# Feature sums of the keys on GpSimd instead of VectorE, in a linear-attention and gated-GLU kernel

## The chip, the cores and the metric

The kernel runs on one core of one Trainium2 chip. The metric is device time in microseconds (us) of one execution; lower is better. Engine names are those of the profile: PE (TensorE, matrix products), PEld (its weight loads), DVE (VectorE), ACT (ScalarE), POOL (GpSimd), SP (SyncE, which issues DMAs).

## The reference, cut to what matters

```
x  = A_x                                     # 1 x 2048 x 512, bf16
xn = layernorm(x)
q, k, v = split(xn @ wqkv)                   # 32 heads of 16
pq, pk  = q @ w_phi, k @ w_phi               # per head, 16 features
phi_q = concat(softmax(pq), softmax(-pq))    # 32 features a head
phi_k = concat(softmax(pk), softmax(-pk))
kv, z = phi_k^T @ v, sum over tokens of phi_k
o   = (phi_q @ kv) / (phi_q @ z + 1e-6)
A   = o @ wo
B   = ((xn @ w_gate) * (xn @ w_up)) @ w_down   # 512 -> 1792 -> 512
out = x + A + B
```

The feature sums are the denominators of the softmaxes. For a tile of 128 tokens there are 32 heads x 2 signs = 64 sums of 16 exponentials each.

## The kernel before

Tokens lie in 16 tiles of 128, one token per partition. All SBUF data lie in one big tensor, which the profile calls arena; all PSUM data in ps, eight banks of 128 x 512 float32.

The stages, as the code records them:

- Layer norm of each tile (`emit_ln_stats`, `emit_xn`): DVE makes statistics (L412, L414), GpSimd adds the epsilon and raises to the power -0.5 (L418, L420), DVE normalises (L434). Tiles 0 to 7 are transposed by PE, tiles 8 to 15 by DMAs on SP (L438).
- Keys. `k_pe` makes the values of a tile; `k_pk` multiplies the normalised tile by a weight in which w_phi is already folded, so that a bank of PSUM holds all 512 features. `emit_exp` copies the bank twice, plain and negated, into one of four slots of the staging ring `pst` (two ACT operations, L276), takes the maximum over the 16 features by a tree of four DVE operations (L474: 512, 256, 128, 64 wide), subtracts it (L480, 1024 wide) and takes the exponential on ACT, into `ek`, 1024 bf16 values per token. `k_norm` then adds up the features by `emit_sums`, takes the reciprocal on DVE (L518) and multiplies the exponentials by it (L521, 1024 wide).
- `emit_sums` is a tree of four additions on halves (L494): 1024 values to 512, to 256, to 128, to 64, each group of 16 features by itself. The inputs of the first are bf16; the partial sums are float32 and lie in the same `pst` slot that the tile's features were in, so a slot becomes free for the tile four places later only when its tree is done.
- `emit_kv`, in two halves of eight tiles, multiplies the transposed normalised key features by the values (and a column of ones, for z): 64 products with 65 columns each. The second half needs all 16 tiles of keys.
- Queries (`q_pk`, `q_scale`, `q_T`, `q_num`, `q_oT`): the same exponentials and the same `emit_sums`, then a ratio, a transposition by DMA, and the products with kv.
- GLU: 56 units (4 groups of 512 tokens x 14 blocks of 128 columns). In `glu` PE makes gate and up, four products each, in two of the banks 5, 6 and 7; ACT copies the gate to SBUF, and DVE multiplies the up bank by it (L543).
- `final` adds for every tile the 14 down products and the 4 with wo in one bank, and DVE adds x (L640).

The order on each engine is not the order of the code. Every operation is recorded with its engine, what it reads and writes, and an estimated cost (`dve`: 65 ns plus 1/0.96 ns per element at rate 1; `pool`: 130 + 1.8 ns per element). Dependencies follow from overlapping addresses. `_order` is a list scheduler: it always starts the operation that can start first by these costs, and among several for one engine the one of the smallest priority number. Matrix products of the GLU have late priorities, so they fill PE's gaps; ACT copies and DVE products of the GLU have the most urgent (-1). The result is one fixed list for each engine. Each engine works its list strictly in order; an operation waits on semaphores for its producers, those on the same engine too (except on PE).

Other instructions named later: L394 makes a block-diagonal weight on GpSimd at the start, four products of 128 elements. L596 to L599 scale the queries. L559 to L566 finish kv. The two lines that set a cost for DVE and for GpSimd:

```python
return sc.step(DVE, fn, reads=reads, writes=writes, cost=fixed + rate * n / 0.96, lat=150.0, prio=prio)   # fixed=65
return sc.step(POOL, fn, reads=reads, writes=writes, cost=fixed + rate * n, lat=120.0, prio=prio)          # fixed=130, rate=1.8
```

Of the kernel before, what the change touches and what calls it, by code (L numbers as in the profile page):

```python
# [8 lines left out]
ALU = mybir.AluOpType  # L9
# [187 lines left out]
def _build(nc, es, A_x, A_wqkv, A_w_phi, A_wo, B_w_gate, B_w_up, B_w_down, out):  # L197
# [59 lines left out]
    def sbv(name, lo, n):  # L257
        off = layout[name] + lo
        return arena[:, off:off + n]
# [25 lines left out]
    def dve(fn, reads, writes, n, rate=1.0, fixed=65.0, prio=None):  # L285
        return sc.step(DVE, fn, reads=reads, writes=writes, cost=fixed + rate * n / 0.96, lat=150.0, prio=prio)
# [196 lines left out]
               func=ACTF.Exp)  # L483
        return i % 4

    def emit_sums(e_in, pslot, slot):

        sm = sums_v[:, slot, :]
        part = sbv("pst", pslot * 1024, 1024).bitcast(F32).rearrange("p (g k) -> p g k", g=16)
        src = e_in.rearrange("p (g k) -> p g k", g=16)  # L490
        k = 32
        while k >= 4:
            dst = part[:, :, 0:k] if k > 4 else sm.rearrange("p (g k) -> p g k", g=16)
            dve(lambda e, dst=dst, src=src, k=k: e.tensor_tensor(out=dst, in0=src[:, :, 0:k], in1=src[:, :, k:2 * k],  # L494
                                                                 op=ALU.add), [src[:, :, 0:2 * k]], [dst], 16 * k)
            src = part
            k //= 2
        return sm

    ek_v = sbv("ek", 0, NT * 1024).rearrange("p (t j) -> p t j", t=NT)  # L500

    p_slot = {}
# [10 lines left out]

    def k_norm(t):
        slot = t % 3
        sm = emit_sums(ek_v[:, t, :], p_slot["k", t], slot)
        rs = rs_v[:, slot, :]
        dve(lambda e: e.reciprocal(out=rs, in_=sm), [sm], [rs], 64, rate=6.0)  # L518
        e4 = ek_v[:, t, :].rearrange("p (g f h) -> p g f h", g=16, f=16)
        r4 = rs.rearrange("p (g h) -> p g h", g=16)  # L520
        dve(lambda e: e.tensor_tensor(out=e4, in0=e4, in1=r4[:, :, None, :].to_broadcast([128, 16, 16, 4]),  # L521
                                      op=ALU.mult), [ek_v[:, t, :], rs], [ek_v[:, t, :]], 1024, rate=0.5)
# [67 lines left out]
    def q_scale(t):  # L590

        slot = t % 3
        sm = emit_sums(eq(t), p_slot["q", t], slot).rearrange("p (g w h) -> p g w h", g=8, w=2)
        rf = rsf_v[:, slot, 0:32].rearrange("p (g h) -> p g h", g=8)
        rs = rs_v[:, slot, 0:32].rearrange("p (g h) -> p g h", g=8)
        dve(lambda e: e.reciprocal(out=rf, in_=sm[:, :, 1, :]), [sm], [rf], 32, rate=6.0)  # L596
        dve(lambda e: e.tensor_tensor(out=rs, in0=sm[:, :, 0, :], in1=rf, op=ALU.mult), [sm, rf], [rs], 32)  # L597
        e1 = eq(t).rearrange("p (g w f h) -> p g w f h", g=8, w=2, f=16)[:, :, 1, :, :]
        dve(lambda e: e.tensor_tensor(out=e1, in0=e1, in1=rs[:, :, None, :].to_broadcast([128, 8, 16, 4]),  # L599
                                      op=ALU.mult), [e1, rs], [e1], 512, rate=0.5)  # L600
# [60 lines left out]
    for b0 in range(0, NT, 4):  # L661
        if b0 < 12:
            ln(b0 + 4, 4)
        if b0 == 8:
            load_wT(0, 0.0).deps.append(sc.by_eng[SP][-2])
            emit_kv(0)
            some_glu(99, 2)
        for t in range(b0, b0 + 4):
            k_pk(t)
            k_norm(t)  # L670
            if b0 < 8:
                some_glu(2, 1)
        if b0 < 12:
            for t in range(b0 + 4, b0 + 8):
                k_pe(t)
        if b0 == 8:
            wprime(0)
# [165 lines left out]
```

## Time and profile before

| what | value |
|---|---|
| median of 3 runs | 226.76 us (226.38 to 228.73) |
| the profiled execution | 227.26 us |
| its span, first to last instruction | 225.5 us |
| granted TensorE clock | 0.999 |
| busy PE / DVE / ACT / POOL | 218.9 / 191.7 / 115.5 / 10.2 us |
| all `emit_sums` additions on DVE (L494) | 128 instructions, 49.3 us, mean 397 ns |
| maxima on DVE (L474) | 128 instructions, 31.5 us, mean 272 ns |
| GLU products on DVE (L543) | 56 instructions, 37.9 us, mean 679 ns |
| first sum of the keys, last multiply of the keys starts | 26.34 us, 113.3 us |

How to read it: busy times of different engines overlap. Instructions of one engine overlap a little too (the recorded length of a DVE instruction is longer than its distance to the next), so both the mean length and the distance between starts are used, and it is said which. A row of section 2 has 40 slices of 5.64 us. "Idle before" a group is the time its engine stood still just ahead of it, and the name behind the arrow is what ended the wait.

### The profile page before, as it was taken

What the parts mean: (1) busy time and instruction counts of PE and PEld (TensorE: products, weight loads), DVE (VectorE), ACT (ScalarE), POOL (GpSimd) and SP (SyncE); (2) the same over time, 40 slices, a digit from 0 to 9 for tenths busy, and PEclk for the clock granted to TensorE, in tenths of its full rate; (3) what the DMA queues carried; (4) which work ended last, traced back from release to release, by engine and by line L of the source; (5) the groups of instructions that cost most, each with busy time, mean ns of one, the idle gap of its engine ahead of it and who ended that gap; (6) DMA issues with size and microseconds to landing.
All of it is one profiled execution on the core that took longest, in us unless ns stands there. A gap on an engine that the chain in (4) does not pass through costs nothing.

```text
span 225.5 us, 3619 instructions
## 1 busy us (share of the span) xinstructions
PE 218.9 (97%) x1312; PEld 106.9 (47%) x1312; DVE 191.7 (85%) x548; ACT 115.5 (51%) x193; POOL 10.2 (5%) x29
## 2 busy tenths in 40 slices
PE   8899999999999999998999999989999999999995
PEld 8454444444455454443454444444444444454443
DVE  4758999999993899999989999989999999974121
ACT  2579976674434998654519765536453333100000
POOL 4721000000020000000000000000000000000000
PEclk9999999999999999999999999999999999999999
DMA  6999931300004400000000044434456643663201
GB/s 163 327 269 400 357 119 28 70 0 0 0 3 95 93 3 0 0 0 3 0 1 3 8 89 89 92 67 78 93 57 110 133 115 76 145 140 73 70 23 48
DMA packets 44210, 19.39 MB, mean 86 GB/s; under 512 B 35232, under 2 KB 43168, under 8 KB 44192
## 3 DMA queue, kind: packets, MB, share of 16 engines
q1 hardware_dynamic: 43664, 19.14, 34.5%
q8 instruction: 10, 0.16, 0.3%
q10 hardware_dynamic: 528, 0.02, 0.1%
q14 instruction: 8, 0.07, 0.1%
HBM read 8.67 MB, written 2.10 MB: 48 GB/s over the span
## 4 chain that ended last, share of the span: by engine, by line
PE 66%; DVE 20%; DMA 5%; SPq 5%; issue 2%; ACT 1%; DVEq 0%
PE ps L296 66%; DVE arena L494 4%; DVE arena L543 4%; DVE arena L474 4%; SPq L163 3%; DMA arena<-in_A_x_dram 3%; DVE arena L480 3%; DMA arena<-arena 2%; SPq L164 1%; DVE arena L412 1%; ACT arena L276 1%; DVE arena L613 1%; DVE arena L518 1%; DVE arena L599 0%; DVE arena L521 0%
## 5 line engine op out<-in xcount | busy, mean ns | idle before, releaser
L296 PE MATMUL ps<-arena 128*128 128x512 bf16 (+4 forms) x1312 | 218.9, 330 | 3.9 <-ACT arena L276 1.1
L296 PEld LDWEIGHTS ps<-arena 128*128 128x128 bf16 x1312 | 106.9, 100 | 115.7 <-ACT arena L276 6.0
L276 ACT ACTIVATE arena<-ps 128x512 bf16<-128x512 f32 (+1 forms) x160 | 84.2, 601 | 47.2 <-PE ps L296 42.3
L276 ACT ACTIVATE arena<-arena 128x1024 bf16<-128x1024 bf16 x32 | 34.3, 1074 | 32.0 <-DVE arena L480 31.1
L494 DVE TENSOR_TENSOR arena<-arena 128x512 f32<-128x512 bf16 (+3 forms) x128 | 49.3, 397 | 0.1
L543 DVE TENSOR_TENSOR arena<-ps,arena 128x512 bf16<-128x512 f32 x56 | 37.9, 679 | 3.4 <-PE ps L296 1.8
L474 DVE TENSOR_TENSOR arena<-arena 128x64 bf16<-128x64 bf16 (+3 forms) x128 | 31.5, 272 | 1.7 <-ACT arena L276 1.6
L640 DVE TENSOR_TENSOR arena<-ps,arena 128x512 bf16<-128x512 f32 (+2 forms) x17 | 11.0, 653 | 12.6 <-PE ps L296 12.5
L480 DVE TENSOR_TENSOR arena<-arena 128x1024 bf16<-128x1024 bf16 x32 | 21.7, 677 | 0.0
L412 DVE BATCH_NORM_STATS2 arena<-arena 128x6 f32<-128x512 bf16 x16 | 10.6, 683 | 4.4 <-DMA arena<-in_A_x_dram 4.4
L521 DVE TENSOR_TENSOR arena<-arena 128x1024 bf16<-128x1024 bf16 x16 | 10.9, 681 | 0.0
L613 DVE TENSOR_TENSOR arena<-ps,arena 128x512 bf16<-128x512 f32 x16 | 10.8, 672 | 0.1
L612 DVE RECIPROCAL arena<-ps 128x32 f32<-128x32 f32 x16 | 5.5, 342 | 4.6 <-PE ps L296 4.5
L518 DVE RECIPROCAL arena<-arena 128x64 bf16<-128x64 f32 x16 | 8.7, 546 | 0.1
L434 DVE TENSOR_SCALAR arena<-arena 128x512 bf16<-128x512 bf16 x16 | 6.2, 416 | 1.9 <-issue 1.5
L599 DVE TENSOR_TENSOR arena<-arena 128x512 bf16<-128x512 bf16 x16 | 6.6, 411 | 0.0
L420 POOL TENSOR_TENSOR arena<-arena 128x1 f32<-128x1 f32 (+1 forms) x7 | 5.4, 777 | 0.4
L596 DVE RECIPROCAL arena<-arena 128x32 f32<-128x32 f32 x16 | 5.4, 336 | 0.0
L418 POOL TENSOR_SCALAR arena<-arena 128x1 f32<-128x1 f32 (+1 forms) x7 | 1.7, 250 | 54.0 <-DVE arena L414 53.9
L597 DVE TENSOR_TENSOR arena<-arena 128x32 bf16<-128x32 f32 x16 | 2.8, 174 | 0.0
L559 DVE TENSOR_TENSOR arena<-ps,arena 128x65 f32<-128x65 f32 x8 | 1.4, 221 | 0.8 <-PE ps L296 0.8
L276 ACT ACT_TABLE_LOAD x1 | 1.3, 1283 | 1.3 <-PEq L828 1.3
(18 smaller groups left out, 9.8 us busy)
## 6 DMA issues: line engine op xcount, KB each, us to landing
out_dram<-arena SPq DMA_DIRECT2D x15, 128.0 KB, 1.9
arena<-in_B_w_down_dram SPq DMA_DIRECT2D x1, 1792.0 KB, 17.1
arena<-in_B_w_gate_dram SPq DMA_DIRECT2D x1, 1280.0 KB, 8.9
arena<-in_B_w_up_dram SPq DMA_DIRECT2D x1, 1280.0 KB, 12.5
arena<-in_A_x_dram SPq DMA_DIRECT2D x1, 1024.0 KB, 6.2
arena<-arena SPq DMA_TRANSPOSE x40, 2.6
arena<-in_A_wqkv_dram SPq DMA_DIRECT2D x1, 512.0 KB, 5.0
arena<-in_A_x_dram SPq DMA_DIRECT2D x1, 512.0 KB, 6.3
```

The lines of the kernel that those rows point to most:

```text
L163: return e.dma_start_transpose(out_ap, in_ap)
L276: return e.activation(out=out_ap, in_=in_ap, func=func, scale=scale, **kw)
L296: ins = e.matmul(o, lhsT=l, rhs=r, start=a, stop=z)
L412: dve(lambda e, t=t: e.bn_stats(stats_v[:, t, 0:6], x_tile(t)), [x_tile(t)], [stats_v[:, t, 0:6]], 512)
L474: dve(lambda e, dst=dst, src=src, k=k: e.tensor_tensor(out=dst, in0=src[:, :, 0:k], in1=src[:, :, k:2 * k], op=ALU.max), [src], [dst], 16 ...
L480: dve(lambda e: e.tensor_tensor(out=p4, in0=p4, in1=src[:, :, None, :].to_broadcast([128, 16, 16, 4]), op=ALU.subtract), [pst, src], [pst] ...
L494: dve(lambda e, dst=dst, src=src, k=k: e.tensor_tensor(out=dst, in0=src[:, :, 0:k], in1=src[:, :, k:2 * k], op=ALU.add), [src[:, :, 0:2 * ...
L518: dve(lambda e: e.reciprocal(out=rs, in_=sm), [sm], [rs], 64, rate=6.0)
L521: dve(lambda e: e.tensor_tensor(out=e4, in0=e4, in1=r4[:, :, None, :].to_broadcast([128, 16, 16, 4]), op=ALU.mult), [ek_v[:, t, :], rs], [ ...
L543: dve(lambda e: e.tensor_tensor(out=dst, in0=bank(bu), in1=gr, op=ALU.mult), [bank(bu), gr], [dst], 512, prio=-1.0)
L613: dve(lambda e: e.tensor_tensor(out=o.rearrange("p (g h d) -> p g h d", g=8, h=4), in0=nd[:, :, 0:64].rearrange("p g (h d) -> p g h d", h= ...
L640: dve(lambda e: e.tensor_tensor(out=og, in0=ob, in1=xs, op=ALU.add), [ob, xs], [og], c1 - c0, prio=-2.0)
```

## The change

`emit_sums` gets an argument `on_pool`. With it the four additions are recorded by `pool` and not by `dve`; `k_norm` sets it, `q_scale` does not. So 64 of the 128 additions (16 tiles of keys x 4) go to GpSimd, with the same operands, shapes and types. Their cost for the scheduler becomes that of `pool`, so all five lists are planned again. A line is added, so that later lines of the changed kernel have numbers higher by one (L494 becomes L495, L518 L519, L521 L522, L543 L544).

```diff
-    def emit_sums(e_in, pslot, slot):
+    def emit_sums(e_in, pslot, slot, on_pool=False):
...
-            dve(lambda e, dst=dst, src=src, k=k: e.tensor_tensor(out=dst, in0=src[:, :, 0:k], in1=src[:, :, k:2 * k],
-                                                                 op=ALU.add), [src[:, :, 0:2 * k]], [dst], 16 * k)
+            op = pool if on_pool else dve
+            op(lambda e, dst=dst, src=src, k=k: e.tensor_tensor(out=dst, in0=src[:, :, 0:k], in1=src[:, :, k:2 * k],
+                                                                op=ALU.add), [src[:, :, 0:2 * k]], [dst], 16 * k)
...
     def k_norm(t):
         slot = t % 3
-        sm = emit_sums(ek_v[:, t, :], p_slot["k", t], slot)
+        sm = emit_sums(ek_v[:, t, :], p_slot["k", t], slot, on_pool=True)
```

In the new lists, PE has 164 products of 512 columns between the last product of 128 columns of the start and the first half of `emit_kv`, where it had 224, and 316 up to the second half, where it had 431. GpSimd's list has the 64 additions mostly interleaved between two neighbouring tiles, in four groups of four tiles; L418 and L420 of tiles 12 to 15 stand inside the second group.

## The prediction, made before the changed kernel ran

> **What bounds the kernel now.** I read the 40 slices first, then the chain that ended last, then stages, forms and the few GpSimd instructions.
>
> ```profile
> span 225.5 us, 3619 instructions
> PE   8899999999999999998999999989999999999995
> DVE  4758999999993899999989999989999999974121
> POOL 4721000000020000000000000000000000000000
> PE 66%; DVE 20%; DMA 5%; SPq 5%; issue 2%; ACT 1%; DVEq 0%
> ```
>
> PE and DVE are both full from the fourth slice to the 36th; DVE has air only at the end. The chain runs through PE for 66% of the span. The stage table cuts at 26.3 us (first sum of the keys), 114.0 (end of the last normalising multiply of the keys) and 147 (PE enters its last unbroken stretch). Its columns are window, sum, then PE, PEld, DVE, ACT and POOL busy with counts, clock, DMA share, GB/s.
>
> ```profile
> 26.30:114.00 87.70, 86.82 (x469) 39.71 (x467) 82.89 (x215) 56.02 (x98) 1.27 (x2) 1.00 0.14 34
> 114.00:147.00 33.00, 32.96 (x229) 16.03 (x226) 31.86 (x111) 20.89 (x34) 0.00 (x0) 1.00 0.25 49
> 147.00:222.50 75.50, 74.72 (x452) 36.50 (x452) 58.03 (x169) 20.60 (x29) 0.00 (x0) 1.00 0.44 90
> ```
>
> PE is idle for 0.88 + 0.04 + 0.78 = 1.7 us after 26.3, at clock 1.00. No PE work is removed, so freeing DVE can win about 1.7 us. Losing is open: DVE empties the banks that PE fills, and PE's order is fixed when the program is built.
>
> The lines that price the change (busy us and mean ns of one, then idle before it):
>
> ```profile
> L494 DVE TENSOR_TENSOR arena<-arena 128x512 f32<-128x512 bf16 x32 | 21.8, 680 | 0.0
> L494 DVE TENSOR_TENSOR arena<-arena 128x256 f32<-128x256 f32 x32 | 13.4, 417 | 0.0
> L494 DVE TENSOR_TENSOR arena<-arena 128x128 f32<-128x128 f32 x32 | 8.7, 273 | 0.0
> L494 DVE TENSOR_TENSOR arena<-arena 128x64 f32<-128x64 f32 x32 | 7.0, 218 | 0.1
> L434 DVE TENSOR_SCALAR arena<-arena 128x512 bf16<-128x512 bf16 x16 | 6.2, 416 | 1.9 <-issue 1.5 <-POOL arena L420 0.2
> L394 POOL TENSOR_TENSOR arena<-arena 128x128 bf16<-128x128 bf16 x4 | 1.6, 401 | 0.3
> ACT arena L276 <- DVE arena L494: 5.3, 6, 1.4
> ```
>
> L394 is the only GpSimd operation of real width with two tensors as inputs; half of the 32 in each L494 row belong to the keys. The last line, of the waits, shows ScalarE already held by these sums: a slot of the staging ring is free only when its tile's tree is done. And these are the meetings of a GpSimd with a DVE instruction (start, length):
>
> ```profile
> 9.14 1.36 POOL L394 TENSOR_TENSOR arena<-arena 128x128 bf16<-128x128 bf16 x3
> 9.64 0.53 DVE L434 TENSOR_SCALAR arena<-arena 128x512 bf16<-128x512 bf16 x1
> 21.70 1.04 POOL L420 TENSOR_TENSOR arena<-arena 128x4 f32<-128x4 f32 x1
> 21.79 0.41 DVE L474 TENSOR_TENSOR arena<-arena 128x512 bf16<-128x512 bf16 x1
> ```
>
> The three L394 start 0.48 apart, so the second is at 9.62 to 10.02. The L434 that began beside it took 0.53 us against 0.41 for its like, ending 0.15 after it. The L474 beside a 4-element L420 took its usual 0.41.
>
> **The change part by part.** *Removed from DVE:* 64 adds. On a full DVE they follow each other, in the chain, at 0.60, 0.34, 0.19 and 0.15 us, 1.28 per tile and 20.5 over 16 tiles (by the row means, which overlap, 25). Little is on the end's path, since PE is 98% busy: gain 0 to 1.7 us; I take 1.7.
>
> *Added on GpSimd:* per tile 512 + 256 + 128 + 64 = 960 elements in four dependent adds. L394 gives 0.40 us for 128 elements; with 0.13 as start-up (the 8-element GpSimd instructions take 0.10 to 0.19) that is 2.1 ns an element, so 1.20, 0.67, 0.40 and 0.26: 2.54 us a tile, 40.6 in all. Upper bound: all of the 0.48 spacing scaled by width, 3.75 ns, 3.6 us a tile. Lower: the affine select's (419 - 194)/120 = 1.9 ns without start-up, 1.8 us. I take 2.54, since L394 is the same operation. The planner lays the order out for 130 + 1.8n, 2.25 us.
>
> *Moved:* the order is planned anew. PE meets the first keys-values products after 164 instead of 224 wide matmuls, and the second after 316 in all instead of 431: 115 x 0.21 us (48 in 10 us) = 24 us earlier. The stage of 87.7 us is thus laid out for about 63, with the GLU work it loses behind it; in total PE has the same. DVE's reciprocal (L519 there) of a tile waits for the fourth GpSimd add, and the GLU products (L544 there), which free PE's banks, queue behind it on DVE. On ACT the copy into the next pst slot waits for GpSimd in place of DVE, with GLU copies behind it. On GpSimd, variance and power of tiles 12 to 15 (L418, L420) are now behind adds of two groups; their DVE normalising and SP transposes follow. SP's other transposes and stores only shift; nothing is issued twice.
>
> *Does GpSimd keep up, running freely?* The ring of four slots makes four groups of four tiles, 10.2 us of GpSimd each. Between a group's first exponential and its fourth reciprocal the new DVE order has work of 11.8, 9.5, 8.3 and 11.2 us (counted by kind: L474 0.34/0.20/0.13/0.10, wide ones 0.60, reciprocal 0.46, L434 0.33). So DVE waits 0.7 + 1.9 = 2.6 us in the second and third group, partly covered: 0 to 2.6, I take 1.
>
> *Do the two engines hinder each other?* This decides. Of that DVE work 6.0, 3.9, 5.7 and 5.6 us, 21.2 together, are additions, maxima or products of two SBUF tensors. Lower end: nothing, as for L474 beside L420, which read only 4 elements. Upper end: one at a time, 21.2 us added. L434 was held 0.12 us of the 0.38 that it lay beside L394, a third; but it is short, and met one add only. With start-up taken off both sides (0.13 on GpSimd; 0.07 on DVE, from 0.34 us at 512 and 0.10 at 64), 32.3 us of GpSimd and 17 of DVE streaming exclude each other: 49.4 against 40.6 of GpSimd alone, 8.8 added if packed perfectly, which a fixed order does not do. Between 8.8 and 21.2 I take 14: L434 nears the low figure, but L480 and L522 stream for most of their 0.60.
>
> The Trainium skill, SBUF — State Buffer, section "SBUF: two separate sides", says that a VectorE operation with two SBUF inputs and a GpSimd operation that reads SBUF take a shared port pair exclusively, the first for its whole instruction. The L434 row agrees with some hold, and the L474 row, unhindered inside an L420, does not agree with "whole". By that rule the collisions would be the full 21.2 us and the time about 244.
>
> *Cover.* GLU uses three banks and a unit fills two (eight matmuls, 1.7 us), so PE can be one bank, 0.85 us, ahead of DVE. One such lead per group covers 3.4 us. Beyond it DVE lateness is PE idleness, and nothing later gives it back.
>
> *Sum* against the profiled execution: 225.5 - 1.7 + 1 + 14 - 3.4 = 235.4 us of span. The profiled run took 227.26, 1.76 more than its span, so 237.2; the median of the runs (226.76) lies 0.5 below it: **236.7 us**. Own range: 226.76 - 1.7 + 8.8 - 3.4 = 230.5 to 226.76 + 2.6 + 21.2 = 250.6.
>
> **The rivals.**
> *A. Side by side, not slower.* The adds run next to DVE as L420 next to L474, at 2.54 us a tile. Then 226.76 - 1.7 + (0 to 2.6) = 225.1 to 227.7, about 226. It decides if collisions stay under 7 us in all: 3.4 covered, 1.7 won, the rest within measurement. For it: the one meeting of two-input operations. Against it: the read there was tiny, and the wide meeting shows a delay.
> The Trainium skill, Advanced Engine Details and Errata, section "VectorE Performance Modes", lists tensor_tensor with one-port modes only and names two-port instructions as those that GpSimd blocks; by it only L434 (2.6 us of the eight in the stage) would collide, and the time would be this rival's, 226 to 228. No run shown here settles between the two pages.
> *B. GpSimd itself is the bound.* At 3.6 us a tile a group takes 14.4 us and overhangs DVE's work by 2.6, 4.9, 6.1 and 3.2, 16.8 us. With collisions of 8.8 to 21.2 and cover of 3.4: 249 to 261, about 255. For it: the adds depend on each other, and 0.48 is the real spacing. Against it: part of that is start-up, and neighbouring tiles can interleave.
> *C. Faster.* PE's weight loads wait 6.0 us for ACT, 1.8 for DMA and 1.7 for L543 in the waits, more than the 1.7 of idle PE. Were half of it real and gone with a freer DVE, 226.76 - 4.7 = 222. Against: most lies under running matmuls, and the last stretch of 75.5 us has DVE air already.
> That the adds do not move is excluded: 64 of them stand in GpSimd's new order and none of the keys' in DVE's.
>
> **How the numbers follow.** Chances: forecast 0.54, A 0.26, B 0.12, C 0.08. A measurement of this kernel tells about 1% from no change, 224.5 to 229.0: faster is C, same is A, slower is forecast and B: 0.08, 0.26, 0.66. From 225.5 to 251, left out are C, the lowest piece of A and most of B, about 0.2 in all. The forecast's own range is 230.5 to 250.6.
>
> **What would show it.** Right: the 512-wide add near 1.2 us on GpSimd; means of L474, L480 and L522 there well above 417 to 183, 677 and 681 while GpSimd runs, and usual afterwards; PE idle, with weight loads waiting for L544 and for ACT, of about 10 us between 26 and 110; from there on the same lengths as before. Rival A: unchanged DVE means and PE as full as now. Rival B: adds near 1.9 us and DVE idle before L519 on GpSimd. The prediction is wrong if GpSimd's adds are priced far from L394, if the two engines do not hinder each other, or if PE finds enough lead that late banks do not stop it.

## The result, and the profile after

The changed kernel takes 240.56 us (median of 6 runs, 239.73 to 241.59) against 226.74 us before (6 runs): a ratio of 1.060, 95% interval 1.057 to 1.063. The forecast was 236.7, in a range from 225.5 to 251. The profiled execution took 240.28 us with a span of 238.5.

The slices of the page after (each now 5.96 us) against those shown of before:

```profile
span 238.5 us, 3617 instructions
PE   6799959997996998779999999999999999999995
DVE  4749999989489799689999999999999984111121
POOL 4522694598019919920000000000000000000000
PE 58%; POOL 16%; DVE 11%; SPq 4%; DMA 4%; ACT 3%; issue 1%; POOLq 0%; DVEq 0%; ACTq 0%
```

GpSimd now works in four blocks, one for each group of four tiles, up to the 18th slice. PE has four holes, one at or near each block, and none afterwards. GpSimd has entered the chain that ended last with 16%. The stages (window, sum, then PE, PEld, DVE, ACT and POOL busy with counts, clock, DMA share, GB/s), cut where the last multiply of the keys ends:

```profile
26.00:104.30 78.30, 67.50 (x360) 28.67 (x359) 68.24 (x137) 48.39 (x86) 52.98 (x66) 0.98 0.18 40
104.30:235.60 131.30, 131.30 (x790) 63.56 (x790) 99.26 (x294) 48.86 (x76) 0.00 (x0) 1.00 0.31 64
```

All the idleness of PE between 26 us and its last product, 78.30 - 67.50 = 10.8 us where it was 1.7, lies in the keys stage. That stage ends at 104.3 where it ended at 114.0: about 10 us earlier, and not the 24 that the new order asks for. The groups of the adds and of the DVE instructions around them, after, inside 26 to 104.3 us for DVE and over the whole run for GpSimd (busy us, mean ns of one):

```profile
L522 DVE TENSOR_TENSOR arena<-arena 128x1024 bf16<-128x1024 bf16 x16 | 14.7, 921 | 0.2
L480 DVE TENSOR_TENSOR arena<-arena 128x1024 bf16<-128x1024 bf16 x14 | 10.9, 780 | 0.0
L519 DVE RECIPROCAL arena<-arena 128x64 bf16<-128x64 f32 x16 | 8.7, 542 | 5.0 <-POOL arena L495 5.0
L474 DVE TENSOR_TENSOR arena<-arena 128x64 bf16<-128x64 bf16 x14 | 5.6, 400 | 0.0
L434 DVE TENSOR_SCALAR arena<-arena 128x512 bf16<-128x512 bf16 x8 | 5.5, 682 | 0.3 <-POOL arena L420 0.3
L474 DVE TENSOR_TENSOR arena<-arena 128x128 bf16<-128x128 bf16 x13 | 5.1, 392 | 0.0
L474 DVE TENSOR_TENSOR arena<-arena 128x512 bf16<-128x512 bf16 x12 | 5.1, 421 | 2.0 <-ACT arena L276 2.0
```

```profile
L495 POOL TENSOR_TENSOR arena<-arena 128x512 f32<-128x512 bf16 x16 | 21.4, 1339 | 26.0 <-ACT arena L276 26.0
L495 POOL TENSOR_TENSOR arena<-arena 128x256 f32<-128x256 f32 x16 | 14.0, 873 | 0.5
L495 POOL TENSOR_TENSOR arena<-arena 128x128 f32<-128x128 f32 x16 | 9.8, 612 | 0.2
L495 POOL TENSOR_TENSOR arena<-arena 128x64 f32<-128x64 f32 x16 | 8.2, 516 | 0.4
```

Against before (681, 677, 183, 406 for L434 in that stage, 211), these DVE means have grown by 240 x 16 + 103 x 14 + 217 x 14 + 276 x 8 + 181 x 13 ns = 3.8 + 1.4 + 3.0 + 2.2 + 2.4 = 12.8 us. The 512-wide maximum (421 ns against 414) and the 256-wide one (277 against 281) have not grown in this order, although both read two halves of a tensor in SBUF. That is no property of theirs: in the real-price kernel below the 512-wide maximum has a mean of 458 ns over all 32, where it had 417. The instructions that read PSUM and the reciprocal, which reads one float32 tensor, have not grown either: the reciprocal is at 542 ns against 546, the GLU product at 673 against 679. L434, which grew most, reads one wide tensor and not two. With the 5.0 us in which DVE stands before its reciprocals, 17.8 of the 20.5 us of DVE time that the adds had taken are gone again. A tree takes GpSimd 1.34 + 0.87 + 0.61 + 0.52 = 3.34 us.

How it happens is seen at the first tile. First DVE, then GpSimd around the same time (start, length), after:

```profile
26.17 1.25 DVE L434 TENSOR_SCALAR arena<-arena 128x512 bf16<-128x512 bf16 x1
27.34 0.68 DVE L480 TENSOR_TENSOR arena<-arena 128x1024 bf16<-128x1024 bf16 x1
27.95 0.75 DVE L474 TENSOR_TENSOR arena<-arena 128x128 bf16<-128x128 bf16 x1
28.62 1.26 DVE L434 TENSOR_SCALAR arena<-arena 128x512 bf16<-128x512 bf16 x1
```

```profile
25.67 1.60 POOL L495 TENSOR_TENSOR arena<-arena 128x512 f32<-128x512 bf16 x1 [3.20 <-ACT arena L276]
27.35 1.27 POOL L495 TENSOR_TENSOR arena<-arena 128x256 f32<-128x256 f32 x1
28.58 1.15 POOL L495 TENSOR_TENSOR arena<-arena 128x512 f32<-128x512 bf16 x1
```

The engines take turns. The add runs to 27.27 and L434, begun at 26.17, ends at 27.42, 0.15 us after it: the distance that the L434 beside L394 had shown before the change. Then L480 runs at its usual length and the 256-wide add beside it takes 1.27 instead of its 0.87 on average; the 128-wide maximum behind L480 takes 0.75 us instead of its usual 0.21 and ends just behind that add (28.70 against 28.62), and so on.

### The profile page after: what moved, and what is told of

Its sections match the earlier page's. It is cut to its first block, busy times and chain, and to the rows that moved or that the text cites. A ratio compares the mean times of both kernels' runs of the same rounds, so it can differ in the third digit from the quotient of the medians.

```text
span 238.5 us, 3617 instructions
## 1 busy us (share of the span) xinstructions
PE 221.6 (93%) x1312; PEld 105.8 (44%) x1312; DVE 186.2 (78%) x484; ACT 114.9 (48%) x193; POOL 62.2 (26%) x93
## 4 chain that ended last, share of the span: by engine, by line
PE 58%; POOL 16%; DVE 11%; SPq 4%; DMA 4%; ACT 3%; issue 1%; POOLq 0%; DVEq 0%; ACTq 0%
PE ps L296 58%; POOL arena L495 16%; ACT arena L276 3%; SPq L163 3%; DMA arena<-in_A_x_dram 2%; DVE arena L474 2%; DVE arena L434 2%; DVE arena L412 2%; DMA arena<-arena 2%; SPq L164 1%; DVE arena L480 1%; DVE arena L544 1%; DVE arena L522 1%; DVE arena L519 1%; POOL arena L420 1%
## 5 line engine op out<-in xcount | busy, mean ns | idle before, releaser
L296 PE MATMUL ps<-arena 128*128 128x512 bf16 (+4 forms) x1312 | 221.6, 330 | 14.2 <-DVE arena L544 7.0
L296 PEld LDWEIGHTS ps<-arena 128*128 128x128 bf16 x1312 | 105.8, 99 | 129.8 <-DVE arena L544 11.2
L276 ACT ACTIVATE arena<-ps 128x512 bf16<-128x512 f32 (+1 forms) x160 | 83.2, 597 | 53.5 <-PE ps L296 47.2
L495 POOL TENSOR_TENSOR arena<-arena 128x512 f32<-128x512 bf16 (+3 forms) x64 | 51.7, 835 | 27.1 <-ACT arena L276 26.0
L544 DVE TENSOR_TENSOR arena<-ps,arena 128x512 bf16<-128x512 f32 x56 | 38.0, 678 | 2.4 <-PE ps L296 2.3
L474 DVE TENSOR_TENSOR arena<-arena 128x64 bf16<-128x64 bf16 (+3 forms) x128 | 36.3, 311 | 2.5 <-ACT arena L276 2.3
L495 DVE TENSOR_TENSOR arena<-arena 128x512 f32<-128x512 bf16 (+1 forms) x64 | 25.2, 398 | 0.1
L480 DVE TENSOR_TENSOR arena<-arena 128x1024 bf16<-128x1024 bf16 x32 | 23.1, 721 | 0.0
L522 DVE TENSOR_TENSOR arena<-arena 128x1024 bf16<-128x1024 bf16 x16 | 14.7, 921 | 0.2
L519 DVE RECIPROCAL arena<-arena 128x64 bf16<-128x64 f32 x16 | 8.7, 542 | 5.0 <-POOL arena L495 5.0
L434 DVE TENSOR_SCALAR arena<-arena 128x512 bf16<-128x512 bf16 x16 | 8.5, 545 | 2.4 <-issue 1.5
L420 POOL TENSOR_TENSOR arena<-arena 128x1 f32<-128x1 f32 (+1 forms) x7 | 5.8, 840 | 0.3
L418 POOL TENSOR_SCALAR arena<-arena 128x1 f32<-128x1 f32 (+1 forms) x7 | 1.7, 248 | 12.3 <-DVE arena L414 12.1
## 6 DMA issues: line engine op xcount, KB each, us to landing
arena<-in_B_w_up_dram SPq DMA_DIRECT2D x1, 1280.0 KB, 12.5
```

The costliest lines, as they stand in the source:

```text
L276: return e.activation(out=out_ap, in_=in_ap, func=func, scale=scale, **kw)
L296: ins = e.matmul(o, lhsT=l, rhs=r, start=a, stop=z)
L434: dve(lambda e: e.tensor_scalar(out=xn_tile(t), in0=x_tile(t), scalar1=mv_v[:, t, 0:1], scalar2=rstd_v[:, t, 0:1], op0=ALU.subtract, op1=A ...
L480: dve(lambda e: e.tensor_tensor(out=p4, in0=p4, in1=src[:, :, None, :].to_broadcast([128, 16, 16, 4]), op=ALU.subtract), [pst, src], [pst] ...
L495: op(lambda e, dst=dst, src=src, k=k: e.tensor_tensor(out=dst, in0=src[:, :, 0:k], in1=src[:, :, k:2 * k], op=ALU.add), [src[:, :, 0:2 * k ...
L544: dve(lambda e: e.tensor_tensor(out=dst, in0=bank(bu), in1=gr, op=ALU.mult), [bank(bu), gr], [dst], 512, prio=-1.0)
```

## The experiments

The theories: **H**, the prediction's, that GpSimd's adds and DVE's instructions with two SBUF inputs hinder each other, and that this takes back what the adds gave; **W**, that GpSimd's adds are slow by themselves and only waiting for them costs; **O**, that the re-planned order is the loss, whoever adds.

**Idle trees.** The kernel before, with the lists of PE, ACT, DVE and SP as they were, and trees on GpSimd beside it whose result nobody uses (the helper is new and lines shift: DVE's adds are L492, its multiply L534, its GLU product L556):

```diff
+    def idle_tree(t, lo, after=None):     # four adds on x into a scratch, as in emit_sums, on POOL
...
     def k_norm(t):
+        idle_tree(t, 4096, sc.by_eng[ACT][-1])   # behind this tile's exponential
...
+    for t in range(8):
+        idle_tree(t, 0)                   # at the end, when the query buffers are free
     for t in range(NT - 1):
         final(t, ...)
```

> The kernel before, unchanged on PE, DVE, ACT and SP (same lists), and in addition GpSimd runs a tree of four adds of the same shapes on idle data (x) once each keys tile's exponential is done, into a scratch nobody reads, and eight more such trees at the end, when DVE has air. DVE keeps its own 64 adds; nothing ever waits for the extra trees. Theory H (the engines hinder each other): DVE's two-SBUF-input instructions and L434 lengthen by about 0.2 us each while GpSimd adds, the time rises by 8 to 20 us to 235 to 247; the eight late trees run at 2.5 us each, well under the 3.34 us measured in the keys stage. Rival W (GpSimd's adds are slow by themselves and only the waiting for them costs): 226.7 us, DVE means as before, late trees at 3.3 us as well. Rival O (the re-planned order): 226.7 us.

Measured: 245.96 us, ratio 1.084 (1.081 to 1.087). Nothing waits for these trees, and no list has moved, so W and O both gave 226.7. DVE in this kernel (whole run, keys and queries together):

```profile
L492 DVE TENSOR_TENSOR arena<-arena 128x512 f32<-128x512 bf16 x32 | 30.2, 944 | 0.0
L492 DVE TENSOR_TENSOR arena<-arena 128x256 f32<-128x256 f32 x32 | 16.1, 504 | 0.0
L534 DVE TENSOR_TENSOR arena<-arena 128x1024 bf16<-128x1024 bf16 x16 | 11.6, 723 | 0.0
L556 DVE TENSOR_TENSOR arena<-ps,arena 128x512 bf16<-128x512 f32 x56 | 37.7, 675 | 3.3 <-PE ps L294 1.8 <-ACT arena L274 1.3
PE ps L294 <- DVE arena L556: 11.7, 14, 2.1
```

DVE's own float32 adds went from 680 to 944 ns, the GLU product did not change, and PE stood 11.7 us for it. The late trees give GpSimd's price when DVE runs only a few instructions that read PSUM (222.8 to 240 us):

```profile
L504 POOL TENSOR_TENSOR arena<-arena 128x512 f32<-128x512 bf16 x6 | 6.9, 1157 | 0.2
L504 POOL TENSOR_TENSOR arena<-arena 128x256 f32<-128x256 f32 x6 | 4.4, 732 | 0.5
L504 POOL TENSOR_TENSOR arena<-arena 128x128 f32<-128x128 f32 x6 | 2.7, 454 | 0.5
L504 POOL TENSOR_TENSOR arena<-arena 128x64 f32<-128x64 f32 x6 | 1.9, 322 | 0.5
```

The four add up to 2.67 us a tree, undisturbed, against 3.34 in the changed kernel. The hindrance goes both ways.

**Memsets.** The same, but GpSimd sets memory and reads none: in `idle_tree`, `e.tensor_tensor(...)` becomes two `e.memset(dst, 0.0)`, and the late trees are left out.

> As the idle trees, but instead of each add GpSimd sets the same elements to zero, twice: it writes SBUF and reads nothing, and nothing waits for it. Theory H, if reading is what collides: 226.7 us within 1%, DVE's two-input means as before. If any GpSimd access to SBUF collides: at least 232 us. Rivals W and O: 226.7 us.

Measured: 226.64 us, ratio 1.000 (0.999 to 1.002). The memsets took 0.52, 0.31, 0.20 and 0.15 us, twice for each add, 2.4 us a tile, in the same places; DVE's adds of 512 stayed at 680 ns. GpSimd being busy and writing beside DVE costs nothing here; what the adds do besides is to read two inputs. (No GpSimd operation that reads one input was run, and the memsets fill 2.4 us a tile where the idle trees beside the keys fill 3.6.) One DVE instruction is an exception, seen below with two memsets.

**Real price.** The planner is told what the adds took:

```diff
+            kw = dict(rate=1.84, fixed=400.0) if on_pool else {}
             op(lambda e, ...: e.tensor_tensor(...), [src[:, :, 0:2 * k]], [dst], 16 * k, **kw)
```

> The changed kernel, with the planner told what the adds took in the changed kernel: 400 ns plus 1.84 ns per element (1342, 871, 636, 518 ns; measured 1339, 873, 612, 516) instead of 130 plus 1.8. PE then has 180 and 348 wide products ahead of the two halves of emit_kv, between the 164 and 316 of the changed kernel and the 224 and 431 of before. Rival O (the order was planned for too small a price): most of the 13.8 us comes back, 226 to 230. Theory H: the waits of L519 for GpSimd go, about 5 us, but DVE's instructions stay lengthened by 12 us in all: 232 to 238.

Measured: 237.14 us, ratio 1.045 (1.041 to 1.048). DVE no longer stands before the reciprocal, and the normalising multiply still takes 842 ns. So planning for a slow GpSimd wins back 3.4 us and not most of 13.8. (The four runs took 235.75 us at clock 1.00, and 236.89, 237.40 and 237.62 at 0.991 to 0.993; the last section comes back to this.)

**Old order.** Planned as before, the keys' adds as DVE work; then those 64 steps are handed to GpSimd's list:

```diff
+    for st in global_order:
+        if st.move:                       # the 64 adds of the keys
+            st.eng = st.lane = POOL
+    new_order = {e: [st for st in global_order if st.eng == e] for e in new_order}
```

> Planned as the kernel before, the keys' adds taken as DVE work; afterwards only these 64 adds are handed to GpSimd's list, so PE, ACT and SP have the very lists of before and DVE that list without the 64 adds. Rival O: the new order was the loss, so 227 to 229. Theory H: DVE loses 20 us of own adds, gains about 12 us of lengthening, and in addition waits for a tree of some 3.3 us where its own took 1.3, with the reciprocal planned right behind it: 230 to 240, with DVE idle before L518 above the 5 us of the changed kernel.

Measured: 228.66 us, ratio 1.008 (1.006 to 1.010), below what H as I wrote it had (230 to 240), and inside what I had written for O (227 to 229). The hindrance is there all the same, and so is the wait:

```profile
L522 DVE TENSOR_TENSOR arena<-arena 128x1024 bf16<-128x1024 bf16 x16 | 12.8, 801 | 0.1
L519 DVE RECIPROCAL arena<-arena 128x64 bf16<-128x64 f32 x16 | 8.7, 545 | 6.5 <-POOL arena L495 6.3
26.00:114.00 88.00, 86.02 (x464) 39.10 (x463) 71.86 (x148) 55.66 (x98) 49.79 (x66) 1.00 0.14 32
```

But in this order DVE needs 71.9 us of the 88 where it needed 83.2 (the prediction's table has 82.89 for nearly the same window), and the slack takes up the rest. So H alone does not set the loss: it also takes an order that has already spent the time that DVE seemed to gain.

**New order, adds on DVE.** The counterpart: planned as the changed kernel, then the 64 steps are handed back to DVE at their planned places, `st.eng = st.lane = DVE`.

> The counterpart of the old order: planned as the changed kernel (the same lists on PE, ACT and SP), afterwards the 64 adds are handed back to DVE at their planned places; GpSimd adds nothing. Theory H (the engines exclude each other, and what DVE was freed of comes back as 12 us of lengthening and 5 us of waits): DVE has 20.4 us of adds instead of those 17, so about as long as the changed kernel or a little longer, 238 to 245 us, with no lengthened instruction. If the changed kernel's loss were mostly GpSimd's slow chain itself, DVE's quicker chain (1.28 against 3.34 us a tile) would bring it back to 227 to 232.

Measured: 240.45 us, ratio 1.061 (1.059 to 1.063), the changed kernel's time. No instruction is lengthened (the multiply, L523 here, is at 676 ns) and GpSimd adds nothing. In the order laid out for GpSimd's help, that help is worth nothing that was measured (240.56 with it, 240.45 without). This table is the core of the case:

| us | keys' adds on DVE | keys' adds on GpSimd |
|---|---|---|
| order of before | 226.7 | 228.7 |
| order of the changed kernel | 240.5 | 240.6 |

**One memset, two memsets.** Is the new order bad in itself, or only without the time it counts on? The changed kernel with its very lists, GpSimd setting memory in place of adding. The sums of the keys are left out.

```diff
-            op(lambda e, ...: e.tensor_tensor(out=dst, in0=..., in1=..., op=ALU.add), ...)
+            op(lambda e, ...: e.memset(dst, 16.0), ...)      # two: a memset of a scratch ahead of it
```

> The changed kernel with its very lists on all engines, but each of the 64 GpSimd adds sets its output to 16 and does not add: the sums of the keys are left out, so the output is another. GpSimd then reads nothing (0.52, 0.31, 0.20 and 0.15 us, 1.2 a tile) and every wait for it stays in the program. Theory H: without collisions DVE's freed 20 us are real and the new order is a good one: no lengthened DVE instruction, 224.5 to 227 us. Rival O (the new order is bad in itself): 235 us or more.

> As with one memset, but GpSimd also sets an idle scratch ahead of each, so that a tree takes 2.8 us (0.52 + 0.52, 0.52 + 0.31, 0.31 + 0.20, 0.20 + 0.15), about the 2.67 us that it takes undisturbed at the end of the idle-trees kernel; the sums of the keys are left out here too. This is GpSimd's length and its waits without collisions, the prediction's rival A. Theory H: 225 to 229 us, with some us of DVE idle before L519 and no lengthened instruction. If the length of GpSimd's chain is what costs: 234 to 240 us.

Measured: 224.80 us, ratio 0.991 (0.989 to 0.992), and 226.35 us, ratio 0.998 (0.996 to 1.000). The kernel before, run beside these two, took 227.04. Two memsets keep GpSimd busy nearly as long as undisturbed adds would (39.5 us in the stage; sixteen trees of 2.67 and 1.3 us of other work would be 44.0), and DVE waits for it (lines shift: L523 is the reciprocal, L526 the multiply, L432 the normalising of a tile that was L434):

```profile
L526 DVE TENSOR_TENSOR arena<-arena 128x1024 bf16<-128x1024 bf16 x16 | 10.9, 684 | 0.2
L523 DVE RECIPROCAL arena<-arena 128x64 bf16<-128x64 f32 x16 | 8.7, 543 | 1.8 <-POOL arena L498 1.7
26.00:104.30 78.30, 77.54 (x479) 36.61 (x477) 69.84 (x193) 57.72 (x102) 39.49 (x130) 1.00 0.21 41
27.77 0.68 DVE L432 TENSOR_SCALAR arena<-arena 128x512 bf16<-128x512 bf16 x1
27.78 0.52 POOL L497 MEMSET arena<- 128x512 f32 x1
```

In the same 78.3 us PE issues 479 products where it issued 360 in the changed kernel, from the same list. The order is good for 224.8 us if DVE's time is really free; a GpSimd of that length costs 226.35 - 224.80 = 1.6 us of it; the collisions, with what they set off, cost the other 240.56 - 226.35 = 14.2 us (up to some tenths of this may be length, since the memsets are a little short). Rivals W and O in their plain form are out.

The last two lines are the exception: L432 took 0.68 us beside a memset, and its eight in this stage have a mean of 482 ns where they had 406 in the kernel before. The multiply beside the same memsets stayed at 684. So setting memory does hinder this one instruction, by 0.6 us in all; DVE's instructions with two inputs it does not hinder.

**Smaller doses.** Only the odd tiles' adds on GpSimd, `on_pool=t % 2 == 1`, in the old order and in the changed kernel; and a plan that also knows the lengthening (fixed costs of the keys' maxima, subtraction and multiply raised by 140, 172, 88 and 240 ns).

> As the old order, but only the odd tiles' 32 adds go to GpSimd. Half of the old order's loss of 0.8%, or less, since DVE catches up in between: 226.3 to 227.8 us. If a relieved DVE is worth anything to PE, 225.3 to 226.2, faster than both kernels.

> The changed kernel with only the odd tiles' adds on GpSimd, planned anew with the planner's own prices; PE has 204 and 376 wide products ahead of the halves of emit_kv. Theory H: half of the adds, half of the lengthening and half of the freed time spent in the plan: 231 to 235 us. If GpSimd's length (over 10 us per group of four) is the bound, a group now takes half and fits beside DVE: 226 to 229.

> The real-price kernel, with the planner also told the lengthening that the changed kernel showed on the keys' DVE instructions: maxima of 128 and 64 by 140 and 172 ns, subtraction by 88, normalising multiply by 240. PE gets 204 and 400 wide products ahead of the two halves of emit_kv (before 224 and 431, changed 164 and 316, real price 180 and 348). Theory H with a plan that spends freed time which is not there: 227.5 to 231 us, close to the old order's 228.7. If waits for GpSimd in the order itself are what is left of the loss: 233 to 237 as with the real price alone.

Measured: 227.11 us, ratio 1.0022 (1.0010 to 1.0034); 232.55 us, ratio 1.026 (1.024 to 1.028); and 231.12 us (median of all four), ratio 1.017 (1.012 to 1.022). Half the adds cost 5.9 us in a new plan and 0.4 in the old one. The four runs of the last one spread: 228.89 and 229.99 at clock 1.00, 232.25 at 0.993, and 233.76, the profiled one and left out of the ratio, at 0.985. With a full clock it comes near the old order's 228.7. None beats the kernel before.

## Why the prediction was right, step by step

- *Adds removed from DVE: gain 1.7 us.* One memset, which leaves DVE relieved and hardly hindered, gains 227.04 - 224.80 = 2.2 us against the kernel before of the same series. Right, if a little small.
- *GpSimd's price: 2.54 us a tree*, taken from four 128-element products. Undisturbed it is 2.67 (1157, 732, 454, 322 ns against 1.20, 0.67, 0.40, 0.26 us). Right within 5%; beside a busy DVE it became 3.34.
- *GpSimd's own length: 0 to 2.6, 1 taken.* 1.6 us by the memsets. Right.
- *The collisions: between 8.8 and 21.2, 14 taken.* DVE lost 12.8 us to lengthening, and its wait for GpSimd grew from 1.8 us (two memsets) to 5.0, 3.2 more: 16.0. The 2.0 us that this is above 14 are nearly the 2.2 us by which L434 grew, which the prediction's 21.2 us of two-input work did not count, although its evidence was an L434. That evidence was in part luck: in the changed kernel's own trace an L434 that began 0.22 us into an L394 (9.67 against 9.45) took its usual 0.40. But the distance of 0.15 us between the two ends is found again beside the wide add. The L474 beside the 4-element L420, which spoke for rival A, was no guide for wide adds.
- *The cover: 3.4 us.* From two memsets to the changed kernel DVE loses 15.4 us (the 16.0 less the 0.6 that L434 had lost there already) and the time grows by 14.2, of which about 1.7 are no DVE time but PE's clock (last section): 15.4 - 12.5 = 2.9. The size is about right, but it is a remainder of other terms. That it is made of one bank of lead in each of the four groups is not shown; PE's wait for L544 is 7.0 us in five pieces, the longest 2.9.
- *The sum.* 236.7 against 240.56, 3.9 us short: the collisions less their cover by 1.9 (12.5 where the sum had 10.6), the clock, which the sum did not have, by 1.7, and GpSimd's length by 0.6, while the larger gain takes 0.5 back.
- *The stage.* That the order brings PE's work forward, and that later stages keep their length, both held: after 104.3 PE has no idle time at all. What I did not say is that the two belong together: the same adds on GpSimd cost 1.9 us in the old order, and the new order costs as much with the adds on DVE.

The rule of the Trainium skill, SBUF — State Buffer, section "SBUF: two separate sides", that a VectorE operation with two SBUF inputs and a GpSimd operation that reads SBUF exclude each other, agrees with the runs: reading GpSimd 245.96 us, writing GpSimd 226.64. Its "whole instruction" fits the wide adds roughly (L434, 0.41 us alone, ends 0.15 us after one), and the estimate that the prediction worked out with it, 244, was nearer than the forecast, by little and without the clock. The Trainium skill's other page, Advanced Engine Details and Errata, section "VectorE Performance Modes", which names only two-port instructions as blocked, does not cover what was measured: tensor_tensor, which it lists without a two-port mode, went from 680 to 944 ns in the idle-trees kernel.

## What to carry to other kernels

Work moved from DVE to GpSimd is not free where the two read SBUF at the same time; here 20.5 us taken off DVE came back as 17.8 us of lengthening and waits. Test it with idle work first: a GpSimd operation nobody waits for, beside an unchanged kernel, shows the price of the collision without any re-planning. And where a planner turns an assumed saving into an order, a saving that does not come is lost again as idle time of the engine whose work was brought forward, here PE: hand the work over in the old order, to see the two apart.

## What the runs showed of the hardware that was not expected

A pause of PE can halve its clock for some microseconds. In the changed kernel PE stands 2.86 us for L544, until 34.56 us. The rows are PE's timeline, then two stretches (clock behind the counts), the second cut where the granted clock is at half:

```profile
34.56 4.65 PE L296 MATMUL ps<-arena 128*128 128x512 bf16 x13 [2.86 <-DVE arena L544]
```

```profile
31.22:34.64 3.42, 0.56 (x4) 0.11 (x2) 3.42 (x7) 2.84 (x5) 3.42 (x5) 1.00 0.63 119
34.64:38.05 3.41, 3.41 (x9) 1.24 (x9) 3.29 (x5) 1.62 (x4) 3.41 (x5) 0.50 0.00 0
```

In 3.41 us at clock 0.50 PE makes nine products; in the next 3.41 us at full clock it makes 18. So the dip costs half of 3.41, about 1.7 us. One such dip in 238.5 us makes a mean clock of 0.993, which all six runs have. In the stretch of the same length just before it, PE was busy for 0.56 us, 16%.

Whether a pause does this hangs on where it falls. In the profiled real-price run PE paused 2.79 us, nearly as long, but across two such stretches, in which it was still busy 1.72 and 2.31 of 3.41 us, and the clock stayed at 1.00. The other three runs of that very kernel have 0.991 to 0.993 and are 1.1 to 1.9 us longer. In the profiled runs with a dip the stretch ahead of it had PE busy for 16% (changed kernel), 28% (the plan that also knows the lengthening) and 38% (new order, adds on DVE); a stretch with 47%, at 74 us of the real-price kernel, was not followed by one. So the edge lay between 38 and 47% in these traces. Coming back took more: a stretch at half clock with PE 66% busy (34.0 to 37.4 us of the plan that also knows the lengthening) was followed by another at half.

The Trainium skill, TensorE: Matmul & The Clock Gate, Part 1, gives an idle window of about 3.4 us that runs freely. The trace agrees with the length, 3.41 us; but PE need not be idle for the whole of it, as the 38% show.

The span grew by 13.0 us. PE's idle time is 10.3 of it (238.5 - 221.6 against 225.5 - 218.9), 9.1 of that after 26 us, and its busy time 2.7, of which the clock is about 1.7; the remaining 1 was not traced further.
